# A second MLP run in four segments instead of three, its weight reloads issued by SyncE, and conversion left out of the steps that end block sums

## The chip, the core and the metric

One core of a Trainium2 chip runs the whole program as one launch. The metric is the device time of that launch in microseconds (us). Each kernel was run several times and the median stands for it.

## The reference, cut to what matters

Attention over 4 batches and 8 heads of 576 tokens comes first, then two MLPs over the 2304 tokens with 512 features. The change touches the second MLP (and one detail of the first).

```python
def _moe_ref(x, w_in, w_out):            # first MLP: 512 -> 2048 -> 512
    h = x @ w_in
    g = h - np.tanh(h)
    return (g @ w_out).astype(np.float32)

def _moe2_ref(x, w_gate, w_val, w_out):  # second MLP: 512 -> 1536 -> 512
    gate = 1.0 / (1.0 + np.exp(-(x @ w_gate)))
    val = x @ w_val
    return (gate * val @ w_out).astype(np.float32)
```

## The kernel before, in words

All weights arrive as 64-bit floats and are converted on the chip to a high and a low 32-bit part; every product is then three matmuls (high by high, low by high, high by low).

**First MLP.** 48 steps of two hidden chunks of 128 each, in an order in which each of 6 token blocks of 384 appears once with the first half of the hidden chunks and once with the second half. A step issues `first` (24 matmuls, line 661) and, for an earlier step, `fifth` (24 matmuls into four sums called acc, line 725). When a block's half ends, `sixth` empties the four sums. In the second half it adds the partial result that had been stored: four adds on VectorE (DVE), line 741. The next block's `fifth` needs these four sums free.

**Conversion of the weights.** `Weights.step` takes one item at a time through DVE (four operations, lines 543 to 547), ScalarE (ACT: an absolute value, line 531, and the high part, line 554) and GpSimd (POOL: the low part, line 552, and sums and differences of weights, line 602). Converted weights of the second MLP go through three staging slots to DRAM (`wsc`, stored by SyncE, SP, on line 607). `W.lag` is the number of slots between the operation that frees or fills a buffer and the place in the program where the DMA for it is issued. In the first MLP one item is converted per step. What is left is converted during the second MLP by `convert()`, one piece per slot, four slots per item.

**Second MLP.** Tokens are taken in 3 groups (tau) of 768, hidden features in 6 chunks (fp) of 256. One pair (tau, fp) is here called a unit, so there are 18. A unit has 14 slots: 7 products for each of its two halves m (a scheme with 7 products in place of 8, lines 862 and 895 to 931). A slot's product is 6 matmuls into one of two PSUM banks. ACT or DVE empties the bank; the first product of a half is emptied by ACT (`e<-sum`, line 906), and the next but one product needs that bank. In 12 of the 14 slots a piece of the down projection of the unit before (3 matmuls, line 878) follows the product; slots 12, 13 and 0 come without one, so in the trace the three of them stand as one block of 18 matmuls of line 862, once per unit.

**Reloads.** A unit needs 9 weight tiles of 512 KB from `wsc`, in a ring of 13 buffers. `feed` issues a load as soon as, in program order, the buffer's last user has been issued. In steady state that gives 7 loads in slot 12 and one each in slots 13 and 0. The 7 are called the burst here. They are weights 2 to 8 of the next unit, the first of them wanted in its slot 2. Once the second MLP runs, `feed` issues them from ACT's queue (line 811), between ACT's other instructions. Every DMA also takes one of eight completion semaphores in turn, so it waits until the DMA that stands eight DMAs before it in the program has landed.

**Change of group.** In the last unit of a group the 14 inputs of the next group are made by `x_next` (line 795): two high parts on ACT and two low parts on POOL and DVE in each of 7 slots. In the unit after it the six finished sums leave through `leave` (line 886) and a store to `out`.

Of the kernel before, what the change touches and what calls it, by code (L numbers as in the profile page):

```python
# [7 lines left out]
F32 = mybir.dt.float32  # L8
# [407 lines left out]
TBS = (None, 384, 384)  # L416
# [25 lines left out]
X0_AT = N1 - 4  # L442
X0_STEPS = (X0_AT + 1, X0_AT + 2, X0_AT + 3)

# [188 lines left out]
def mlps(tc, st, xr, x0, W, xs, x2s, out, consts):  # L633
# [158 lines left out]
    def x_make(j, kp, low):  # L792
# [5 lines left out]
          X0_AT + 2: ([(0, 3), (1, 3)], [(6, 0), (6, 1), (7, 0), (7, 1), (5, 0)]),  # L798
          X0_AT + 3: ([], [(5, 1), (4, 0), (4, 1), (3, 0), (3, 1)])}

    loads = [(tau, fp, i) for tau in range(NPAIR) for fp in range(NFP) for i in range(PER_FP)]
    ring, held, issued, spent = [], {}, [0], set()

    def feed():
        while issued[0] < len(loads):
            k = issued[0]
            tau, fp, i = loads[k]
            if (fp, i) not in W.stored or k >= len(ring) and (k < RING_SLOTS or loads[k - RING_SLOTS] not in spent):
                return
            w = W.slot(ring[k % RING_SLOTS])  # L810
            (nc.scalar if s > SLOTS2 // 2 else nc.sync).dma_start(w.bitcast(F32).rearrange("p a c -> p (a c)"), W.wsc[fp][i])  # L811
            held[loads[k]] = w
            issued[0] += 1
# [4 lines left out]
    def convert():  # L818
        while W.made <= W.n:
            highs, lows, mixes, conv = W.step()  # L820
            for f in conv[:2]:
                f()
                yield
            for f in highs + lows:
                f()
            for f in conv[2:]:
                f()
                yield
            for f in mixes:
                f()  # L830
            W.scan()
            if not conv:
                yield
# [13 lines left out]
    def mat(s):  # L847
        g, j = divmod(s, GROUPS2)
        u, m = divmod(g, 2)
        tau, fp = divmod(u, NFP)  # L850
        return tau, fp, m, j

    def product(s):
        tau, fp, m, j = mat(s)
        w = held[tau, fp, j]
        p = banks[s % 2]
        fresh = j in (0, 1, 4)
        for kp in range(2):
            x = xw[PRODUCTS[j], kp]
            for i, (a, c) in enumerate(P3):  # L860
                o = 256 * m + 128 * kp
                T.matmul(p, w[:, a, o:o + 128], x[:, c], start=(fresh and kp == 0 and i == 0),  # L862
                         stop=(kp == 1 and i == 2), skip_group_check=True)
        if m:
            spent.add((tau, fp, j))

    def down():
        if not downs:
            return
        tau, fp, f, key, d, last = downs.pop(0)  # L870
        h, l = res[key]
        w = held[tau, fp, GROUPS2 + f]
        t = key[-1]
        begin = fp == 0 and f == t
        end = fp == NFP - 1 and f != t
        c = slice(128 * d, 128 * d + 128)
        for i, (g, a) in enumerate(((h, 0), (h, 1), (l, 0))):
            T.matmul(sums[3 * t + d], g[:, c], w[:, a], start=(begin and i == 0), stop=(end and i == 2))  # L878
        if last:
            spent.add((tau, fp, GROUPS2 + f))  # L880
        if end:
            return lambda: leave(tau, t, d)

    def leave(tau, t, d):
        o = ob.tile([128, DM], F32, name="o")
        (V.tensor_copy if d % 2 else A.copy)(o, sums[3 * t + d])
        r = TP * tau + TB * t + 128 * d
        nc.sync.dma_start(out[r:r + 128, :], o)
# [10 lines left out]
    def evacuate(s):  # L899
        tau, fp, m, j = mat(s)  # L900
        p = banks[s % 2]
        u = tau, fp
# [27 lines left out]
    def finish(s, u, f, t, q, gate):  # L930
        key = (*u, f, t)
        d = 0 if gate is None else 1
        if d:
            at(s + 1, lambda: G.tensor_mul(q, q, gate))
        c = s + 1 + d
        if f == 0 and t == 1:
            c = max(c, s + 5)
        at(c, lambda: cast(key, q))
        at(c + 1, lambda: lower(key, q))

        def queue():
            for i in range(3):
                downs.append((*u, f, key, i, i == 2 and (f, t) in ((1, 0), (0, 1))))
        order = {(0, 0): 0, (1, 1): 1, (1, 0): 2, (0, 1): 3}[f, t]
        at(SLOTS2 * ((u[0] * NFP) + u[1] + 1) + 3 * order - 1, queue)

    def slot2(s):
        tau, fp, m, j = mat(s)
# [9 lines left out]
        if tau + 1 < NPAIR:  # L958
# [20 lines left out]
    for n in range(N1 + 3):  # L979
# [8 lines left out]
        if 2 <= n < N1 and n not in X0_STEPS:  # L988
# [12 lines left out]
        if n == N1:  # L1001
# [7 lines left out]
            W.lag = 2  # L1009
# [36 lines left out]
    while s < SLOTS2 * NPAIR * NFP:  # L1046
# [19 lines left out]
def tile_attention_then_two_mlps(ctx: ExitStack, tc: tile.TileContext, qT, kT, vP, par, wi, wo, wg, wv, wo2, c_log, ident, out, xs=None):  # L1066
# [5 lines left out]
    x2s = dp.tile([DM, NT], F32, name="x2s")  # L1072
    wsc = [[dp.tile([128, 1024], F32, name=f"wsc{i}_{j}") for j in range(PER_FP)] for i in range(NFP)]
    with tc.manual_schedule():
# [27 lines left out]
        m = mlps(tc, ctx, xr, x0, W, xs, x2s, out, cst)  # L1102
# [75 lines left out]
```

## Time and profile before

| | |
|---|---|
| time, median of 3 runs | 1190.41 us (1187.73 to 1194.6) |
| profiled execution: its own time | 1193.65 us |
| profiled execution: span of the trace | 1191.8 us |
| TensorE matmul busy | 1127.8 us, 95% of the span |
| DVE, ACT, POOL busy | 794.0, 660.6 and 651.7 us |
| mean granted TensorE clock | 0.987 |
| DMA moved | 225.64 MB, mean 189 GB/s |

The span runs from the first to the last instruction. Attention and the biases take about the first 340 us, the first MLP ends near 750 us, and the second MLP fills the rest. A busy share is a mean over all of them, so the stretches have to be read apart.

### The profile page before, as it was taken

The numbers are of one execution on the slowest core, as the hardware profiler recorded it, in microseconds if no ns is written. First come the engines' busy times: TensorE is split into PE (matmuls) and PEld (weight loads), VectorE is DVE, ScalarE is ACT, GpSimd is POOL, SyncE is SP. The second block draws the span as 40 slices with busy tenths as digits, with TensorE's granted clock in tenths as the row PEclk, the third lists the DMA queues.
The fourth block names the chain that finished last, engine by engine and source line by source line (L and its number), as shares of the span: only waits on it lengthen the run. The fifth ranks groups of instructions, "written<-read, shape, count | busy, mean of one in ns | idle before, by whom it ended". The sixth has DMA issues, their size and how long they took to land.

```text
span 1191.8 us, 19819 instructions
## 1 busy us (share of the span) xinstructions
PE 1127.8 (95%) x6968; PEld 980.9 (82%) x6968; DVE 794.0 (67%) x1401; ACT 660.6 (55%) x1313; POOL 651.7 (55%) x588
## 2 busy tenths in 40 slices
PE   5679999999999999999999999988999999999998
PEld 1246676767689999999999999887888998889997
DVE  8979888888579988898899885773242332432222
ACT  7877787778657776677676755433242212421122
POOL 1047777777545655697787954866352223522332
PEclk9889999999999999999999999999999999999999
DMA  6654546363223332367756777976565545664452
GB/s 211 239 185 138 168 141 193 112 200 102 78 72 110 108 107 97 111 230 237 248 190 206 245 249 279 351 292 272 231 241 225 200 159 218 242 228 160 169 232 94
DMA packets 103026, 225.64 MB, mean 189 GB/s; under 512 B 12176, under 2 KB 52368, under 8 KB 102928
## 3 DMA queue, kind: packets, MB, share of 16 engines
q1 hardware_dynamic: 81472, 146.25, 36.8%
q10 hardware_dynamic: 21456, 78.13, 17.1%
q8 instruction: 56, 0.92, 0.3%
q14 instruction: 42, 0.34, 0.1%
HBM read 166.26 MB, written 58.08 MB: 188 GB/s over the span
## 4 chain that ended last, share of the span: by engine, by line
PE 76%; DMA 6%; ACT 5%; DVE 4%; issue 4%; POOL 3%; ACTq 1%; SPq 0%; DVEq 0%; POOLq 0%
PE sum L862 19%; PE acc L725 13%; PE up L661 13%; PE acc L878 8%; PE sc L227 6%; PE pv L319 6%; PE pt L269 6%; PE up L878 3%; DMA w<-wsc 2%; POOL w L552 2%; DMA bsc<-e 1%; ACTq L811 1%; DMA wsc<-w 1%; PE pv L316 1%; PE bt L75 1%
## 5 line engine op out<-in xcount | busy, mean ns | idle before, releaser
L862 PE MATMUL sum<-w,w 128*128 128x384 f32 x1512 | 306.6, 342 | 21.6 <-ACT e L906 12.9
L862 PEld LDWEIGHTS sum<-w,w 128*128 128x128 f32 x1512 | 272.4, 190 | 49.4 <-ACT e L906 19.8
L661 PE MATMUL up<-xt,w 128*128 128x384 f32 x1152 | 208.5, 335 | 0.3 <-DVE t L695 0.3
L661 PEld LDWEIGHTS up<-xt,w 128*128 128x128 f32 x1152 | 200.1, 188 | 2.9 <-issue 2.2
L725 PE MATMUL acc<-gh,w 128*128 128x384 f32 x768 | 195.8, 335 | 4.2 <-DVE o L741 2.5
L259 POOL TENSOR_SCALAR n<-n,rec 128x576 f32<-128x576 f32 x144 | 121.0, 854 | 83.0 <-ACT n L248 41.0
L706 POOL TENSOR_TENSOR gl<-t,gh 128x384 fp32r<-128x384 f32 x96 | 105.3, 1117 | 93.1 <-issue 39.0
L552 POOL TENSOR_TENSOR w<-wu,w 128x512 fp32r<-128x512 f32 x86 | 129.0, 1512 | 29.8 <-ACT w L554 15.0
L725 PEld LDWEIGHTS acc<-gh,w 128*128 128x128 f32 x768 | 138.0, 188 | 6.7 <-ACT xt L651 3.3
L897 POOL TENSOR_TENSOR gl<-e,gh 128x384 fp32r<-128x384 f32 x54 | 57.8, 1074 | 147.0 <-ACT gh L699 146.9
L725 PE MATMUL acc<-gl,w 128*128 128x384 f32 x384 | 128.3, 334 | 0.0
L241 DVE CUSTOM_DVE_ANT_0 n<-sc,bias 128x576 f32<-128x576 f32 x144 | 103.7, 753 | 31.4 <-PE sc L227 26.2
L248 ACT ACTIVATE n<-n,mn 128x576 f32<-128x576 f32 x144 | 111.4, 783 | 8.7 <-DVE mn L241 8.6
L699 ACT CAST gh<-t 128x384 fp32r<-128x384 f32 x114 | 57.7, 515 | 93.3 <-DMA w<-wsc 70.2
L878 PE MATMUL acc<-w,gh 128*128 128x512 f32 x288 | 91.6, 399 | 0.0
L690 ACT ACTIVATE z<-z,c 128x768 f32<-128x768 f32 x48 | 45.2, 941 | 76.3 <-DVE up L689 76.2
L269 PE MATMUL pt<-ident,n 128*128 128x128 f32 x576 | 80.4, 281 | 1.4 <-ACT at L299 1.3
L691 DVE TENSOR_TENSOR t<-up,t 128x768 f32<-128x768 f32 x48 | 45.9, 957 | 53.0 <-ACT t L678 52.4
L319 PE MATMUL pv<-at,vs 128*64 128x320 f32 (+1 forms) x512 | 79.3, 421 | 0.0
L909 DVE TENSOR_TENSOR e<-sum,e 128x384 f32<-128x384 f32 x35 | 19.5, 556 | 89.6 <-ACT e L906 47.2
L923 DVE TENSOR_TENSOR e<-sum,e 128x384 f32<-128x384 f32 x70 | 38.9, 556 | 57.1 <-PE sum L862 57.1
L652 POOL TENSOR_TENSOR xt<-xm,xt 128x384 fp32r<-128x384 f32 x48 | 49.8, 1059 | 44.5 <-ACT xt L651 44.1
(109 smaller groups left out, 2117.2 us busy)
## 6 DMA issues: line engine op xcount, KB each, us to landing
w<-wsc ACTq DMA_DIRECT2D x149, 512.0 KB, 7.8
wsc<-w SPq DMA_DIRECT2D x54, 512.0 KB, 4.9
wraw<-in_wo SPq DMA_DIRECT2D x28, 512.0 KB, 4.3
bsc<-e SPq DMA_DIRECT2D x36, 295.5 KB, 3.1
xm<-xs SPq DMA_DIRECT2D x48, 192.0 KB, 3.3
x2s<-o SPq DMA_DIRECT2D x48, 192.0 KB, 3.7
wraw<-in_wi SPq DMA_DIRECT2D x16, 512.0 KB, 4.2
w<-wsc SPq DMA_DIRECT2D x13, 512.0 KB, 5.6
```

Source lines behind the costliest of these rows:

```text
L227: T.matmul(sc[u, t][:, hf, 0:288], q[r, 128 * s:128 * s + 128], k[r, o:o + 288], start=(i == 0), stop=(i == 2))
L241: V.tensor_tensor_reduce(n.rearrange("p (a b) -> p a b", a=2), s[:, :, 0:288], bias[t].rearrange("p (a b) -> p a b", a=2), -0.125, 3.0e38, ...
L248: A.activation(n, n, AF.Exp, bias=m, scale=-1.0, accum_out=nsum[u, t // 4][:, t % 4:t % 4 + 1])
L259: G.tensor_scalar(n, n, nrec[u, t // 4][:, t % 4:t % 4 + 1], 1.0, ALU.mult, ALU.mult)
L269: T.transpose(pt[:, i], n[:, o:o + 128], ident)
L319: T.matmul(p[0][64 * a:64 * a + 64, 0:N], v[:, c - 1, a], main[:, c - 1, a * N:a * N + N], start=False, stop=(c == 4))
L552: self.nc.gpsimd.tensor_sub(w[:, 1], x, w[:, 0].bitcast(F32))
L661: T.matmul(p[:, 0:TB], w[:, a, 128 * kt:128 * kt + 128], x[:, c], start=(kt == 0 and i == 0), stop=(kt == 3 and i == 2))
L706: G.tensor_sub(l, x[:, j], h.bitcast(F32))
L725: T.matmul(ac[blk][d][:, 0:TB], w[:, a, 128 * d:128 * d + 128], c, start=(begin and j == 0 and i == 0), stop=(end and j == NPR - 1 and i = ...
L862: T.matmul(p, w[:, a, o:o + 128], x[:, c], start=(fresh and kp == 0 and i == 0), stop=(kp == 1 and i == 2), skip_group_check=True)
L878: T.matmul(sums[3 * t + d], g[:, c], w[:, a], start=(begin and i == 0), stop=(end and i == 2))
```

## The change

1. The second MLP runs in four segments (`SEGS`): group 0 with chunks 0 to 2, group 1 with all six chunks, group 2 with all six, group 0 again with chunks 3 to 5. The six sums of the first segment are stored to a DRAM tensor `y2s`; `bring` loads them back in the last unit, and `leave` adds them on DVE. There are still 18 units. The inputs of group 0 are made twice, so there are three changes of group instead of two.
2. All reloads are issued by SP.
3. The steps of the first MLP in which sums of a second half fall due convert nothing (4 steps). So 54 of 68 items, not 58, are made when the second MLP begins, and 14 are left instead of 10.
4. `convert()` yields once more per item: five slots per item in place of four. `W.lag` is 3 slots instead of 2 in the second MLP.
5. Two differences and two input tiles of group 0 are made one step later.

```diff
+SEGS = ((0, 0, 3), (1, 0, NFP), (2, 0, NFP), (0, 3, NFP))
+PAIRS = [(g, tau, fp, fp - lo, hi - lo) for g, (tau, lo, hi) in enumerate(SEGS) for fp in range(lo, hi)]
...
-          X0_AT + 2: ([(0, 3), (1, 3)], [(6, 0), (6, 1), (7, 0), (7, 1), (5, 0)]),
-          X0_AT + 3: ([], [(5, 1), (4, 0), (4, 1), (3, 0), (3, 1)])}
-    loads = [(tau, fp, i) for tau in range(NPAIR) for fp in range(NFP) for i in range(PER_FP)]
+          X0_AT + 2: ([], [(6, 0), (6, 1), (7, 0), (7, 1), (5, 0)]),
+          X0_AT + 3: ([(0, 3), (1, 3)], [(5, 1), (3, 0), (3, 1)]),
+          N1: ([], [(4, 0), (4, 1)])}
+    loads = [(u, i) for u in range(len(PAIRS)) for i in range(PER_FP)]
...
-            (nc.scalar if s > SLOTS2 // 2 else nc.sync).dma_start(w.bitcast(F32).rearrange("p a c -> p (a c)"), W.wsc[fp][i])
+            nc.sync.dma_start(w.bitcast(F32).rearrange("p a c -> p (a c)"), W.wsc[fp][i])
...
             W.scan()
-            if not conv:
-                yield
+            yield
...
+    def leave(g, t, d):
+        tau, lo, hi = SEGS[g]
+        r = TB * t + 128 * d
+        if lo:
+            o = kept.pop((t, d))
+            V.tensor_add(o, sums[3 * t + d], o)
+        else:
+            o = ob.tile([128, DM], F32, name="o")
+            (V.tensor_copy if d % 2 else A.copy)(o, sums[3 * t + d])
+        nc.sync.dma_start(out[TP * tau + r:TP * tau + r + 128, :] if hi == NFP else y2s[r:r + 128, :], o)
+
+    def bring(i):
+        t, d = divmod(i, 3)
+        o = ob.tile([128, DM], F32, name="o") if i < 4 else x0.tile([128, TP], F32, name="xt")[:, 0:DM]
+        nc.sync.dma_start(o, y2s[128 * i:128 * i + 128, :])
+        kept[t, d] = o
...
-            if fp == 1 and m == 0 and j < 4:
-                src_load(tau + 1, j)
-            if fp == 2 and j < 3:
+            if p == n - 3 and m == 1 and j < 4:
+                src_load(SEGS[g + 1][0], j)
+            if p == n - 2 and j < 3:
                 combine(m, j)
-            if fp == NFP - 1 and m == 1:
+            if p == n - 1 and m == 1:
                 x_next(j)
+        elif p == n - 1 and m == 0 and j < 6:
+            bring(j)
...
-        if 2 <= n < N1 and n not in X0_STEPS:
+        if 2 <= n < N1 and n not in X0_STEPS and not any(ends(m) and block(m)[2] for m in due(n - 1, 2)):
             h, low, mixes, conv = W.step()
...
-            W.lag = 2
+            W.lag = 3
```

How instructions move shows at three places. The first is ACT at a unit's end in the steady part, before. Lines 699 and 925 are casts and sigmoids of the hidden features, L811 the weight reloads, L906 the copy that empties a PSUM bank.

```order
L925 ACTIVATE e<-e 128x384
L699 CAST gh<-e 128x384
L811 DMA w_10998<-wsc_2_93 128x1024
L811 DMA w_11000<-wsc_3_94 128x1024
L811 DMA w_11002<-wsc_4_95 128x1024
L811 DMA w_11004<-wsc_5_96 128x1024
L811 DMA w_11006<-wsc_6_97 128x1024
L811 DMA w_11008<-wsc_7_98 128x1024
L811 DMA w_11010<-wsc_8_99 128x1024
L811 DMA w_11020<-wsc_0_100 128x1024
L699 CAST gh<-t 128x384
L811 DMA w_11033<-wsc_1_101 128x1024
```

Now the same place holds no DMA (the same casts and sigmoids, lines 701 and 939, and the copy L920):

```order
L939 ACTIVATE e<-e 128x384
L701 CAST gh<-e 128x384
L701 CAST gh<-t 128x384
L920 COPY e<-sum_9038 128x384
L701 CAST gh<-e 128x384
```

What moved: the nine reloads of a unit have left ACT's program, and the cast of line 701 follows the one before it directly.

The second place is SP in the third unit of the changed kernel, while weights are still being converted: L516 loads raw weights, L609 stores converted ones, L815 reloads.

```order
L609 DMA wsc_5_106<-w_9618 128x1024
L609 DMA wsc_3_104<-w_9619 128x1024
L516 DMA wraw<-in_wg 128x2x256
L516 DMA wraw<-in_wv 128x2x256
L815 DMA w_9745<-wsc_2_67 128x1024
L815 DMA w_9747<-wsc_3_68 128x1024
L815 DMA w_9749<-wsc_4_69 128x1024
L815 DMA w_9751<-wsc_5_70 128x1024
L815 DMA w_9753<-wsc_6_71 128x1024
L815 DMA w_9755<-wsc_7_72 128x1024
L815 DMA w_9757<-wsc_8_73 128x1024
L815 DMA w_9778<-wsc_0_74 128x1024
```

Before, SP's program holds there only raw loads (L514, L518) and stores (L607):

```order
L607 DMA wsc_4_104<-w_9407 128x1024
L607 DMA wsc_2_102<-w_9408 128x1024
L514 DMA wraw<-in_wg 128x2x256
L514 DMA wraw<-in_wv 128x2x256
L607 DMA wsc_1_101<-w_9474 128x1024
L607 DMA wsc_7_107<-w_9475 128x1024
```

What moved: nine reloads per unit now stand in SP's one queue between the stores and raw loads of the conversion, and what comes after them in the program is issued after them.

The third place is DVE in a step of the first MLP that empties four sums of a second half, before. The operations on up and t belong to the activation, those on wu convert weights, and L741 are the four adds.

```order
L689 SCALAR_TENSOR_TENSOR up<-z,up 128x2x384
L547 SCALAR_TENSOR_TENSOR wu<-wraw,wu 128x512
L694 SCALAR_TENSOR_TENSOR up<-q,up 128x2x384
L543 SCALAR_TENSOR_TENSOR wu<-wraw,wu 128x512
L695 COPY_PREDICATED t<-z,up 128x768
L741 TENSOR_TENSOR o<-acc,o 128x384 x4
```

And now:

```order
L693 TENSOR_TENSOR t<-up,t 128x768
L694 SCALAR_TENSOR_TENSOR up<-z,up 128x2x384
L691 SCALAR_TENSOR_TENSOR up<-z,up 128x2x384
L696 SCALAR_TENSOR_TENSOR up<-q,up 128x2x384
L697 COPY_PREDICATED t<-z,up 128x768
L743 TENSOR_TENSOR o<-acc,o 128x384 x4
```

What moved: no operation on wu stands ahead of the four adds in such a step.

## Rows read from the trace of the kernel before

**Rows 1.** The page, part 1: busy time, share of the span, instructions.
```profile
PE 1127.8 (95%) x6968; PEld 980.9 (82%) x6968; DVE 794.0 (67%) x1401; ACT 660.6 (55%) x1313; POOL 651.7 (55%) x588
```

**Rows 2.** Waits of TensorE from 500 us on: total, times, longest.
```profile
PE sum L862 <- ACT e L906: 12.9, 13, 2.8
PE sum L862 <- DVE e L923: 6.6, 4, 2.2
PE acc L725 <- DVE o L741: 2.5, 3, 1.2
```

**Rows 3.** Timeline of TensorE, line 862: start, length, count of matmuls.
```profile
743.54 7.49 PE L862 MATMUL sum<-w,w 128*128 128x384 f32 x42
...
774.82 3.30 PE L862 MATMUL sum<-w,w 128*128 128x384 f32 x18
...
801.67 3.30 PE L862 MATMUL sum<-w,w 128*128 128x384 f32 x18
...
832.76 3.30 PE L862 MATMUL sum<-w,w 128*128 128x384 f32 x18
...
880.57 3.69 PE L862 MATMUL sum<-w,w 128*128 128x384 f32 x18
...
935.11 3.30 PE L862 MATMUL sum<-w,w 128*128 128x384 f32 x18
...
1030.51 3.69 PE L862 MATMUL sum<-w,w 128*128 128x384 f32 x18
...
1082.55 3.30 PE L862 MATMUL sum<-w,w 128*128 128x384 f32 x18
...
1153.69 3.30 PE L862 MATMUL sum<-w,w 128*128 128x384 f32 x18
...
1176.89 2.26 PE L862 MATMUL sum<-w,w 128*128 128x384 f32 x12
```

**Rows 4.** Timeline, 1020 to 1062 us, ACT's DMA queue and TensorE (idle before, releaser).
```profile
1030.70 3.58 ACTq L811 DMA_DIRECT2D w<-wsc  x7
1034.38 0.51 ACT L795 CAST w<-xt 128x384 fp32r<-128x384 f32 x1 [3.86 <-DMA w<-wsc]
...
1036.90 1.33 PE L862 MATMUL sum<-w,w 128*128 128x384 f32 x6 [2.01 <-DVE e L923]
```

**Rows 5.** Windows: length, busy of each engine, granted clock, DMA share, GB/s.
```profile
1036.00:1064.00 28.00, 26.74 (x129) 24.44 (x129) 8.94 (x16) 7.98 (x17) 10.46 (x10) 0.94 0.57 213
```

**Rows 6.** Timeline of ACT, 770 to 830 us.
```profile
775.02 3.73 ACTq L811 DMA_DIRECT2D w<-wsc  x7
...
782.87 0.48 ACT L906 COPY e<-sum 128x384 f32<-128x384 f32 x1 [2.48 <-DMA w<-wsc]
...
801.87 4.08 ACTq L811 DMA_DIRECT2D w<-wsc  x7
...
818.79 1.20 ACT L554 CAST w<-wu 128x512 fp32r<-128x512 f32 x2 [4.50 <-POOL wu L602]
```

**Rows 7.** The chain that ended last, 797 to 810 us: start, length, what.
```profile
802.51 7.23 DMA wsc<-w
```

**Rows 8.** Timelines of the first MLP, 606 to 617 us, TensorE then DVE.
```profile
606.83 4.32 PE L661 MATMUL up<-xt,w 128*128 128x384 f32 x24
612.36 0.59 PE L725 MATMUL acc<-gh,w 128*128 128x384 f32 x2 [1.21 <-DVE o L741]
616.63 4.32 PE L661 MATMUL up<-xt,w 128*128 128x384 f32 x24
...
609.90 0.92 DVE L543 SCALAR_TENSOR_TENSOR wu<-wraw,wu 128x512 int32<-128x512 int32 x1
...
611.67 1.94 DVE L741 TENSOR_TENSOR o<-acc,o 128x384 f32<-128x384 f32 x4
```

**Rows 9.** DMA issues: of 1100 to 1115 us, then of the whole span.
```profile
w<-wsc ACTq DMA_DIRECT2D x9, 512.0 KB, 8.2
...
wsc<-w SPq DMA_DIRECT2D x54, 512.0 KB, 4.9
```

More of the change, by code (lines that the diff above doesn't have):

```diff
@@ L630, in zip_run, with mlps @@
                 x[i]()
-def mlps(tc, st, xr, x0, W, xs, x2s, out, consts):
+def mlps(tc, st, xr, x0, W, xs, x2s, y2s, out, consts):
     nc = tc.nc
@@ L806, in feed @@
             k = issued[0]
-            tau, fp, i = loads[k]
+            u, i = loads[k]
+            fp = PAIRS[u][2]
             if (fp, i) not in W.stored or k >= len(ring) and (k < RING_SLOTS or loads[k - RING_SLOTS] not in spent):
@@ L849, in mat @@
         u, m = divmod(g, 2)
-        tau, fp = divmod(u, NFP)
-        return tau, fp, m, j
+        return u, m, j
     def product(s):
-        tau, fp, m, j = mat(s)
-        w = held[tau, fp, j]
+        u, m, j = mat(s)
+        w = held[u, j]
         p = banks[s % 2]
@@ L864, in product @@
         if m:
-            spent.add((tau, fp, j))
+            spent.add((u, j))
     def down():
@@ L869, in down @@
             return
[L870 to L875, printed above, removed]
+        u, f, t, d, last = downs.pop(0)
+        g, tau, fp, at_, n = PAIRS[u]
+        h, l = res[u, f, t]
+        w = held[u, GROUPS2 + f]
+        begin = at_ == 0 and f == t
+        end = at_ == n - 1 and f != t
         c = slice(128 * d, 128 * d + 128)
-        for i, (g, a) in enumerate(((h, 0), (h, 1), (l, 0))):
-            T.matmul(sums[3 * t + d], g[:, c], w[:, a], start=(begin and i == 0), stop=(end and i == 2))
+        for i, (x, a) in enumerate(((h, 0), (h, 1), (l, 0))):
+            T.matmul(sums[3 * t + d], x[:, c], w[:, a], start=(begin and i == 0), stop=(end and i == 2))
         if last:
-            spent.add((tau, fp, GROUPS2 + f))
+            spent.add((u, GROUPS2 + f))
         if end:
[L882 to L888, printed above, removed]
+            return lambda: leave(g, t, d)
+    def leave(g, t, d):
[8 more added lines that the diff above has]
+        nc.sync.dma_start(out[TP * tau + r:TP * tau + r + 128, :] if hi == NFP else y2s[r:r + 128, :], o)
+    kept = {}
+    def bring(i):
[3 more added lines that the diff above has]
+        kept[t, d] = o
     grp = {}
@@ L899, in evacuate @@
     def evacuate(s):
-        tau, fp, m, j = mat(s)
+        u, m, j = mat(s)
         p = banks[s % 2]
-        u = tau, fp
         if j == 0:
@@ L930, in finish @@
     def finish(s, u, f, t, q, gate):
-        key = (*u, f, t)
+        key = u, f, t
         d = 0 if gate is None else 1
@@ L942, in queue @@
             for i in range(3):
-                downs.append((*u, f, key, i, i == 2 and (f, t) in ((1, 0), (0, 1))))
+                downs.append((u, f, t, i, i == 2 and (f, t) in ((1, 0), (0, 1))))
         order = {(0, 0): 0, (1, 1): 1, (1, 0): 2, (0, 1): 3}[f, t]
-        at(SLOTS2 * ((u[0] * NFP) + u[1] + 1) + 3 * order - 1, queue)
+        at(SLOTS2 * (u + 1) + 3 * order - 1, queue)
     def slot2(s):
-        tau, fp, m, j = mat(s)
+        u, m, j = mat(s)
+        g, tau, fp, p, n = PAIRS[u]
         W.tick()
@@ L957, in slot2 @@
             f()
-        if tau + 1 < NPAIR:
-            if fp == 1 and m == 0 and j < 4:
-                src_load(tau + 1, j)
-            if fp == 2 and j < 3:
+        if g + 1 < len(SEGS):
+            if p == n - 3 and m == 1 and j < 4:
+                src_load(SEGS[g + 1][0], j)
+            if p == n - 2 and j < 3:
                 combine(m, j)
-            if fp == NFP - 1 and m == 1:
+            if p == n - 1 and m == 1:
                 x_next(j)
+        elif p == n - 1 and m == 0 and j < 6:
+            bring(j)
     def x_next(j):
@@ L1045, in mlps @@
     conv = convert()
-    while s < SLOTS2 * NPAIR * NFP:
+    while s < SLOTS2 * len(PAIRS):
         slot2(s)
@@ L1072, in tile_attention_then_two_mlps @@
     x2s = dp.tile([DM, NT], F32, name="x2s")
+    y2s = dp.tile([2 * TBS[2], DM], F32, name="y2s")
     wsc = [[dp.tile([128, 1024], F32, name=f"wsc{i}_{j}") for j in range(PER_FP)] for i in range(NFP)]
@@ L1101, in tile_attention_then_two_mlps @@
         xr, x0 = (ctx.enter_context(tc.tile_pool(name=n, bufs=k)) for n, k in (("p2r", 2), ("p2x0", 4)))
-        m = mlps(tc, ctx, xr, x0, W, xs, x2s, out, cst)
+        m = mlps(tc, ctx, xr, x0, W, xs, x2s, y2s, out, cst)
         def tail(h):
```

## The prediction

> **What bounds the kernel now.** I began with the busy shares [rows 1]: TensorE is at 95%, no other engine above 67%. So other engines matter only where they make TensorE wait, and what can be won at all is TensorE's idle time and the time it runs at a lower granted clock. The table of TensorE's waits says where it idles in the second half [rows 2]: it waits for the copy on ACT that empties a PSUM bank (12.9 us in 13 waits), for DVE's adds that do the same (6.6 us) and, in the first MLP, for the four adds that empty the block sums (2.5 us in 3 waits). No row of that table names a DMA: a reload is never what TensorE itself waits for.
>
> The idle time alone is too small, since after an idle stretch the clock is lower. So I measured whole units: each unit has one block of 18 matmuls, and the distance from block to block is the unit's length [rows 3]. The last two blocks stand 1176.89 - 1153.69 = 23.2 us apart. That is the floor: 14 products of 1.05 us and 12 down pieces of 0.70 us make 23.1. The first block of interest starts at about 743.54 + 5 x 1.05 = 748.8. Over 17 units the second MLP then loses, against 23.2 a unit:
>
> - 748.8 to 832.76, 3 units, weights still being converted: 84.0 - 69.6 = 14.4
> - 832.76 to 880.57, 2 units: 1.4
> - 880.57 to 935.11, 2 units, change of group and the sums' leaving: 8.1
> - 935.11 to 1030.51, 4 units: 2.6
> - 1030.51 to 1082.55, 2 units, the other change of group: 5.6
> - 1082.55 to 1153.69, 3 units: 1.5
>
> Together 33.6 us. What causes it is seen in a change of group [rows 4]. ACT's queue issues the burst of seven loads in 3.58 us; the eighth has to wait for the completion of an earlier load, and the next cast on ACT starts only when that DMA has landed, after 3.86 us idle. ACT works in order, so the inputs of the next group come late, DVE behind them comes late, and TensorE stands for 2.01 us. In the 28 us that follow the mean granted clock is 0.94 [rows 5], so about an eighth of them, some 3 us, passed at the lower level, 1.2 instead of 2.4 GHz, and cost about 1.7 us more. In the conversion the same thing happens [rows 6]: seven issues at 775.02, then ACT's copy of a bank at 782.87, released by a DMA; again at 801.87. At 818.79 the cause is another: ACT waits 4.50 us for POOL's arithmetic on weights.
>
> **The change, part by part.**
>
> *Reloads off ACT.* The nine issues per unit, and the waits between them, go to SP, which computes nothing. The nine steady units (1.4 + 2.6 + 1.5 = 5.5 us) should fall nearly to the floor; I leave 0.5. The two changes of group (13.7 us) keep their work: 14 casts of 0.51 us [rows 4] on ACT, and as many subtractions shared by POOL and DVE, in the seven slots of half a unit, some 12 us. I leave 1 us each, 2 in all. In the conversion I count the loss of 774.82 to 801.67 (26.85 - 23.2 = 3.65) and half of that of 801.67 to 832.76 (31.09 - 23.2 = 7.9, half is 3.8, for the burst at 801.87) to this cause; 7 of the 14.4 stay. What hides the loads afterwards: the first weight of a burst is wanted after the three products of the block (3.2 us), two down pieces and one product, 5.6 us after the issue, and it lands 3.7 us after (1030.70 to 1034.38) [rows 4]. So there is a margin of 1.9 us. Without it, each microsecond of lateness is one of TensorE.
>
> *What SP's one queue now carries.* During the conversion, raw loads and converted stores stand among the reloads, in two ways. A store issued behind a burst lands late: nine loads have a median of 8.2 us to landing [rows 9], the first lands after 3.7, so the last at about 12.7. A store that lands in 4.9 alone [rows 9], and took 7.23 beside a burst in the other queue [rows 7], may take 10 to 15. The staging slot stays taken and ACT's high part waits. By the order of the changed kernel that happens to two of the stores, each with two slots of normal slack. Conversely two bursts stand directly behind two stores and a raw load, some 3 x 1.1 us of transfer (from 8.2 - 3.7 over four loads) against the margin of 1.9. I put 1 us on each of the four, 4 in all; bounds 0 (the slack takes it) and 12 (3 each).
>
> The Trainium skill, "DMA: Bandwidth & Descriptors", "Issuing engines are not separate DMA queues", says that issuing DMAs on several engines only saves the sequencer's issue time, usually small beside the DMA. Read so, taking the loads off ACT would return little; here the trace differs, because 3.58 us of issues and 3.86 us of waiting stand in ACT's program [rows 4]. By the rule alone the steady and group terms would stay as they are.
>
> *Slower conversion, spread wider.* Group 0 stops after chunk 2, so chunks 3 to 5 are wanted at unit 6 instead of unit 3, and an item may take five slots (8.8 us) instead of four (7.0). POOL gets a quarter more time for each, which should ease waits like that of 818.79; but 14 items are left instead of 10. Of the 7 us I keep 5 (bounds 2, if the pace cures it, and 10, if each item costs as before: 7 x 14/10). The store's lag grows from two slots to three, which takes back most of the added room for a staging slot's round trip.
>
> *A third change of group.* The first one now falls into the conversion, where POOL has both the subtractions and the weights. It has no ACT issues, so it need not cost what the two old ones cost; it cannot be free either. I take 3 (bounds 0 and 6.9, half of 13.7).
>
> *First MLP.* In the four steps of line 741 that are changed, DVE loses its four conversion operations, of which one alone takes 0.92 us just ahead of the adds [rows 8]. The stalls are 1.21 us and less, so they should vanish: -2.5 [rows 2]. The four items come back as part of the 14.
>
> *The rest.* TensorE has the same count of products. Six stores and six loads of 256 KB and four of 384 KB are 4.6 MB beside 225 and lie under the products. The last six sums now all leave through DVE, by an add where a copy stood; the chain at the end grows by about 0.3. The two moved differences and input tiles cost nothing as long as POOL is idle where they go; bound 1.
>
> **Sum.** Losses after: 0.5 + 2 + 5 + 3 + 4 + 0.3 = 14.8 instead of 33.6, so -18.8; with the first MLP -21.3. The profiled execution took 1193.65 us, so 1172.3; it lies 3.2 above the median of the runs, 1190.41, which gives 1169.
>
> **The rivals.**
>
> *The conversion eats it.* Two-part items follow each other through three staging slots exactly where the first change of group lies. With all three uncertain terms at their upper bounds (10, 6.9, 12 instead of 5, 3, 4) the sum is 16.9 us worse: -4.4, and 1186. Halfway is 1178. For it: POOL's 4.50 us wait [rows 6]; against: five slots per item. Chance of 1176 to 1184: 0.20.
>
> *ACT's issues only hid the transfers.* The stall of a change of group [rows 4] ends when a DMA lands. If TensorE would then wait for the same load, the 19.2 us of steady units and group changes stay, and what is left is the first MLP (-2.5) and the 2 us that the slower pace takes off the conversion: -4.5, so 1186. Against it: steady units lose no more than half a microsecond each while the same bursts run [rows 3], and no wait of TensorE is on a DMA [rows 2]. The skill's rule above would give this time. Chance 0.09, together with other ways of ending within 0.5%, which is about what a measurement of this kernel can tell from no change.
>
> *Slower: one queue, in order.* SP waits for a low part from POOL before it issues a store, and the burst behind it waits too. This can happen in five units of conversion and three in which sums leave. Without the 4 us for the queue, the change gives 25.3; so it turns into a loss when each of these 8 units waits longer than 3.2 us, idle and slow clock together. At 4 us each, 32 us, the time is 1197. The Trainium skill, same page, "Queues, rings and completion order", supports the shape of it: SP and ACT own one row of rings each, and descriptors of one ring are taken in order. No run here shows yet how far that delays a burst. For it: the store of 7.23 us [rows 7]; against: the loads are in the queue 5.6 us ahead. Chance 0.06.
>
> *Better.* Slack takes up all new terms: conversion 2, group change 0, queue 0 give -31, and 1159. Chance of below 1162: 0.03.
>
> **How the numbers follow.** My forecast, 1169, stands for the case 1162 to 1176 with chance 0.62. Faster by over 0.5% (below 1184.5): 0.62 + 0.20 + 0.03 = 0.85; within 0.5%: 0.09; slower: 0.06. The range 1158 to 1183 takes in the likeliest case and the second and leaves out the two that end near or above the old time.
>
> **What would show it.** In the profile after: no DMA issue on ACT in the second MLP; steady blocks of 18 matmuls 23.2 to 23.4 us apart; the two later changes of group within 2 us of the floor; adds of the block sums in the first MLP without a wait before them in the four steps; a total loss in the first five units below 15 us. Wrong would be: waits of TensorE on a reload, ACT's line for the high parts waiting on a store (the queue), POOL's row full in the third and fourth unit (the conversion), or group changes that still cost 4 us a unit without ACT's issues (then ACT's queue was not the cause).

## The result and the profile after

The changed kernel takes 1173.66 us (median of 4 runs, 1170.99 to 1175.9) against 1191.24 us for the kernel before in the same runs: the ratio is 0.9852, with a 95% interval of 0.9816 to 0.9888. It is faster by 1.5%. The profiled execution took 1173.8 us, its span is 1172.0 us.

The busy shares on the page have hardly moved (compare [rows 1]):

```profile
PE 1123.8 (96%) x6968; PEld 983.2 (84%) x6968; DVE 816.5 (70%) x1422; ACT 666.6 (57%) x1327; POOL 661.2 (56%) x595
```

TensorE's table of waits from 500 us on has (compare [rows 2]; the operations are the same, only the line numbers have moved: L927 is the sigmoid on ACT that empties a bank, L933 and L937 are adds on DVE that do):

```profile
PE sum L864 <- ACT e L927: 4.4, 1, 4.4
PE sum L864 <- DVE t L933: 2.1, 1, 2.1
PE sum L864 <- DMA w<-wsc: 1.8, 1, 1.8
PE sum L864 <- DVE t L937: 1.1, 1, 1.1
PE sum L864 <- DVE e L929: 1.0, 1, 1.0
```

The 12.9 us of waits on ACT's bank copy are gone, and one wait of 4.4 us on ACT's other bank-emptying operation, the sigmoid, has come; the waits in the first MLP are gone; a wait on a reload is new. The timeline of the unit blocks shows where the time is lost now (compare [rows 3]):

```profile
736.72 7.47 PE L864 MATMUL sum<-w,w 128*128 128x384 f32 x42
...
773.03 3.30 PE L864 MATMUL sum<-w,w 128*128 128x384 f32 x18
...
828.02 3.33 PE L864 MATMUL sum<-w,w 128*128 128x384 f32 x18
...
878.04 3.30 PE L864 MATMUL sum<-w,w 128*128 128x384 f32 x18
...
901.24 3.30 PE L864 MATMUL sum<-w,w 128*128 128x384 f32 x18
...
947.64 3.67 PE L864 MATMUL sum<-w,w 128*128 128x384 f32 x18
...
971.21 3.30 PE L864 MATMUL sum<-w,w 128*128 128x384 f32 x18
...
1157.16 2.26 PE L864 MATMUL sum<-w,w 128*128 128x384 f32 x12
```

The unit's length is the distance from block to block, and 23.2 us is the floor that the prediction found. From 878.04 on, 12 units take 279.1 us, 0.7 more than 12 times 23.2. The two changes of group there cost 0.37 us each (947.64 to 971.21 is 23.57). Before, the same kinds of units lost 5.5 and 13.7 us. All the rest is lost earlier. The first block begins at 736.72 + 5.25 = 742.0; the unit to 773.03 loses 7.9 us, the two to 828.02 lose 8.6, the two to 878.04 lose 3.6. That is 20.1 us in these first five units (called the conversion stretch here), where the kernel before lost 14.4 + 1.4 = 15.8.

The whole balance between the two profiled executions: 1.4 us are scatter of the unchanged part (the first of the paired steps of the first MLP starts at 345.60 instead of 347.03); the first MLP from there to the first block is 5.4 us shorter (396.4 instead of 401.8); the second MLP loses 20.8 instead of 33.6, which is 12.8; the end after the last block is the same (14.8 and 14.9 us). Together 19.7, and the executions differ by 19.85.

The chain that ended last shows the first of the three losses, the one of 4.43 us idle (start, length, what):

```profile
745.33 10.32 DMA wsc<-w
755.65 0.02 issue
755.67 0.04 ACTq L556
...
755.75 0.07 ACT w L556
...
756.27 0.49 ACT e L927
...
756.81 2.29 PE sum L864 x6
```

A store of converted weights needs 10.32 us. The high part of the next item (L556) waits on ACT for its staging slot, and the sigmoid that empties a bank (L927) stands behind it in ACT's order. After the idle time six matmuls take 2.29 us, and the windows show the granted clock for the three stretches:

```profile
742.00:773.00 31.00, 26.19 (x121) 23.12 (x120) 21.90 (x30) 8.73 (x18) 21.19 (x16) 0.89 0.82 308
773.00:828.00 55.00, 50.40 (x241) 45.29 (x240) 42.62 (x56) 25.49 (x52) 45.38 (x34) 0.94 0.84 309
828.00:878.00 50.00, 48.20 (x241) 44.35 (x240) 27.69 (x44) 17.04 (x34) 33.20 (x27) 0.97 0.81 308
878.00:948.00 70.00, 70.00 (x364) 65.09 (x363) 25.98 (x45) 19.32 (x40) 26.51 (x27) 1.00 0.61 236
```

A mean of 0.89 means that about a fifth of that window passed at 1.2 GHz; the idle time that TensorE's table names for it is 4.4 of the 7.9 us. In the second stretch, the first change of group, the chain runs through DVE:

```profile
791.02 1.78 DVE wu L549
...
793.19 1.16 DVE w L797
794.35 1.43 DVE wu L545
...
797.05 2.84 DVE xt L792 x2
...
801.08 1.23 DVE wu L547
```

The conversion (wu) and the subtractions of the change (w, xt) alternate on DVE without a gap, and the banks' adds stand between them. POOL has no gap there either, from 789.66 to 802.02 us. In the third stretch TensorE waits 1.80 us for a reload that took 5.63 us (829.84 to 835.47). It is the first of a burst, and SP had issued two stores, a partial sum and a raw load in the 3.3 us ahead of it.

### The profile page after: what moved, and what is told of

Its sections match the earlier page's. It is cut to its first block, busy times and chain, and to the rows that moved or that the text cites. A ratio compares the mean times of both kernels' runs of the same rounds, so it can differ in the third digit from the quotient of the medians.

```text
span 1172.0 us, 19922 instructions
## 1 busy us (share of the span) xinstructions
PE 1123.8 (96%) x6968; PEld 983.2 (84%) x6968; DVE 816.5 (70%) x1422; ACT 666.6 (57%) x1327; POOL 661.2 (56%) x595
## 4 chain that ended last, share of the span: by engine, by line
PE 86%; DMA 4%; DVE 3%; ACT 3%; issue 2%; POOL 1%; SPq 0%; DVEq 0%; ACTq 0%; POOLq 0%
PE sum L864 22%; PE acc L727 16%; PE up L663 16%; PE acc L880 8%; PE sc L227 6%; PE pv L319 6%; PE pt L269 5%; PE up L880 4%; DMA bsc<-e 1%; ACT y L62 1%; PE pv L316 1%; ACT e L86 1%; DMA wsc<-w 1%; PE bt L75 1%; PE pf L273 1%
## 5 line engine op out<-in xcount | busy, mean ns | idle before, releaser
L937 DVE TENSOR_TENSOR e<-sum,e 128x384 f32<-128x384 f32 x70 | 38.8, 556 | 56.1 <-PE sum L864 55.9
L269 PEld LDWEIGHTS pt<-ident,n 128*128 128x128 f32 x576 | 63.8, 142 | 12.6 <-issue 11.4
```

The source lines that it names most:

```text
L269: T.transpose(pt[:, i], n[:, o:o + 128], ident)
```

## The experiments

Each kernel was timed in turn with the kernel before. "Loss" is that of the second MLP in the profiled execution, worked out as above: from the first block to the last, less 17 times 23.2 us. "ACT on store" is ACT's waiting for a staging slot, the row `ACT w <- DMA wsc<-w` of its waits from 716 to 940 us. Both are read from one execution each, while the executions of one kernel lie up to 8 us apart (e7: 1175.54 to 1183.59), so a difference of a few us between two losses is not resolved by itself. The kernel before differs by up to 3 us between the rows as well, so times are compared by their ratios.

| kernel | median us | ratio to before (95%) | loss | ACT on store |
|---|---|---|---|---|
| changed kernel | 1173.66 | 0.9852 (0.9816 to 0.9888) | 20.8 | 9.1 |
| e1, reloads on ACT | 1208.05 | 1.0152 (1.0125 to 1.0178) | 55.4 | 4.6 |
| e2, before with reloads on SP | 1174.24 | 0.9865 (0.9840 to 0.9891) | 15.4 | 3.6 |
| e3, pause at the change | 1183.49 | 0.9956 (0.9936 to 0.9976) | 28.6 | 25.9 |
| e4, conversion in the sum steps | 1173.09 | 0.9856 (0.9826 to 0.9886) | 15.5 | 18.6 |
| e5, two rings | 1169.99 | 0.9854 (0.9836 to 0.9872) | 17.9 | 7.8 |
| e6, stores on POOL | 1179.34 | 0.9930 (0.9913 to 0.9946) | 25.0 | 17.8 |
| e7, three segments | 1177.43 | 0.9922 (0.9892 to 0.9952) | 22.0 | 18.4 |
| e8, inputs as before | 1175.74 | 0.9899 (0.9878 to 0.9920) | 20.1 | 8.8 |
| r9, six slots | 1167.06 | 0.9812 (0.9769 to 0.9854) | 13.4 | 21.3 |
| r10, e3 + e5 + later input loads | 1177.70 | 0.9892 (0.9860 to 0.9924) | 24.9 | 22.8 |
| r11, r10 with six slots | 1163.10 | 0.9774 (0.9751 to 0.9798) | 9.9 | 21.1 |
| r12, r11 with four staging slots | 1161.05 | 0.9753 (0.9739 to 0.9767) | 7.4 | none |

**e1: everything but the queue.**
```diff
-            nc.sync.dma_start(w.bitcast(F32)...
+            (nc.scalar if s > SLOTS2 // 2 else nc.sync).dma_start(w.bitcast(F32)...
```


> The changed kernel with the reloads of the second MLP issued from ACT's queue again; segments, pace, lag and the steps without conversion stay. Theory (ACT's issues and waits cost the time): the steady units and the two late changes of group lose again what they lost before, about 18.5 us (1.4 + 8.1 + 2.6 + 5.6 + 1.5 less the 0.7 that is left), so about 1192 us if the conversion stretch stays as it is, a little less if the stores in a queue of their own land earlier. Rival (the new order of units and the slower pace did it, the queue is indifferent): 1174 us, within 4.

It is slower than the kernel before by 1.5%, and by 34 us than the changed kernel; the last twelve units lose 28.6 us (885.65 to 1192.65) where the changed kernel loses 0.7. The direction is the theory's and the rival is out. The size is larger than either number. ACT's own timeline and the chain show why at the place of the largest loss: eight issues are spread over 10 us and the ninth follows at 897.40, because four of the nine each wait until an input load on SP's queue has landed, the last of which takes 10.06 us. In the trace each of the four has the same completion semaphore as the load that it waits for.

```profile
885.84 10.05 ACTq L815 DMA_DIRECT2D w<-wsc  x8
895.94 0.51 ACT L701 CAST gh<-t 128x384 fp32r<-128x384 f32 x1 [12.64 <-DMA w<-wsc]
...
887.26 10.06 DMA xt<-x2s
...
897.37 0.04 issue
897.40 0.33 ACTq L815
...
897.77 0.49 ACT e L920
...
898.30 1.97 PE sum L864 x5
```

By the times in the two traces, ACT's issues in the second MLP were held until an earlier DMA had landed 13 times here, 26.8 us together, and 6 times, 9.6 us together, in the kernel before.

So the other parts of the change, without the queue's move, cost 19 us (1208.05 against 1188.74 for the kernel before in the same runs).

**e2: the queue alone.**
```diff
-            (nc.scalar if s > SLOTS2 // 2 else nc.sync).dma_start(w.bitcast(F32)...
+            nc.sync.dma_start(w.bitcast(F32)...
```


> The kernel before with one line changed: reloads from SP's queue. Three segments, four slots per item, lag 2, conversion in every step. Theory: the stretch behind the conversion falls to the floor, 15 to 18 us less than before; the conversion stretch loses its ACT issues but gets stores behind bursts, so its 14.4 us become anything from 10 to 20: 1171 to 1181 us. Rival (only the four segments leave room for the conversion): the conversion stretch gets worse by more than 10 us and the whole gain is under 8, above 1183 us.

One changed line gives the same time as the whole change (the intervals of the ratios overlap nearly fully), inside the theory's band. Its waits in the first MLP are about those of before ([rows 2] has the first of them), and its second MLP loses 15.4 us, 14.7 of them in the first five units, less than the changed kernel:

```profile
PE sum L862 <- ACT e L906: 5.9, 1, 5.9
PE acc L725 <- DVE o L741: 2.5, 3, 1.2
...
PE acc L725 <- ACT w L795: 1.8, 1, 1.8
```

**e4: the four items converted in the first MLP after all.** The condition that skips `W.step` is taken out.
```diff
-        if 2 <= n < N1 and n not in X0_STEPS and not any(ends(m) and block(m)[2] for m in due(n - 1, 2)):
+        if 2 <= n < N1 and n not in X0_STEPS:
```


> The changed kernel, converting in the four steps of the first MLP in which the block sums fall due, as before the change; 10 items are then left for the second MLP instead of 14. Theory: TensorE waits for the four adds again, 3 to 4 us in the first MLP; but the conversion in the second MLP has four items less and ends 20 slots earlier, which takes 0 to 6 us off its 20. So 1170 to 1177 us. Rival (the skipped steps are worth what the first MLP gained, and the items cost nothing later): 1177 us.

The ratio is that of the changed kernel. The first MLP's waits of 2.5 us on the adds are back and the first block starts 5.2 us later (747.1), while the loss after it is 5.3 us smaller (15.5). What the first MLP gains by leaving four items out, the second pays for them, as far as one execution can tell. The theory is borne out, the rival (1177) is not.

**e8: the moved differences and inputs.** The table `X0` as before the change.

> The changed kernel with the two differences and two input tiles of group 0 made where they were made before the change. Theory (the moved work freed the wait of 1.0 us before the last block sums of the first MLP): that wait comes back, TensorE's waits in the first MLP sum to about 1 us instead of 0, and the time grows by 1 us, 1173 to 1176 us. Rival (this move cost and saved nothing, as I had predicted): 1173.7 us and no wait in the first MLP.

TensorE's wait on ACT's input tile is back with 1.0 us, as the theory had it. In the time, the intervals overlap; this size is not resolved.

**e7: group 0 in one piece.**
```diff
-SEGS = ((0, 0, 3), (1, 0, NFP), (2, 0, NFP), (0, 3, NFP))
+SEGS = ((0, 0, NFP), (1, 0, NFP), (2, 0, NFP))
...
-            yield
+            if not conv:
+                yield
```
(with the input loads and differences at chunks 1 and 2, and no `bring`)

> The changed kernel with group 0 in one piece again: three segments and four slots per item; reloads on SP, no conversion in the sum steps and lag 3 stay. Theory (the segments only make room, and the room is not what was short): the conversion stretch loses between 14 and 24 us, 1169 to 1179 us, so within 5 us of the changed kernel. Rival (the room counts): with 14 items at four slots each the weights come too late for their unit and TensorE waits for reloads, above 1182 us.

The loss is 22.0 us, 1.2 more than with four segments and five slots, and the two profiled executions lie 2.75 us apart; no wait of TensorE is on a reload, so the rival is out. How little the segments and the fifth slot are worth is less sure: the ratios lie 0.7% apart, some 8 us, and their intervals just miss each other. Against e2, too, e7 is slower (0.9922 and 0.9865, intervals that just miss each other): with three segments, the skipped steps, the lag and the moved inputs together gain nothing.

**e3: no conversion during the first change of group.**
```diff
-        if s > SLOTS2 // 2:
+        if s > SLOTS2 // 2 and not 2 * SLOTS2 + GROUPS2 <= s < 3 * SLOTS2:
             next(conv, None)
```


> The changed kernel, with no piece of conversion in the seven slots of the first change of group; it ends seven slots later, still ahead of where the weights are wanted. Theory (DVE has the group's subtractions and the conversion at once in those slots): the 8.6 us lost between 773 and 828 us fall to 2 to 4, so 1167 to 1170 us. Rival (the change of group costs this by itself, as before the change): 1173 us, the loss stays within 2 us of 8.6.

Both theories missed: 1183.5 us. The change itself is cured, as this theory said: the two units from 770.04 to 817.27 lose 0.8 us, where the changed kernel lost 8.6. But the timeline of TensorE shows two new stalls:

```profile
770.04 3.30 PE L864 MATMUL sum<-w,w 128*128 128x384 f32 x18
...
793.25 3.67 PE L864 MATMUL sum<-w,w 128*128 128x384 f32 x18
...
817.27 3.71 PE L864 MATMUL sum<-w,w 128*128 128x384 f32 x18
...
836.14 2.29 PE L864 MATMUL sum<-w,w 128*128 128x384 f32 x6 [7.39 <-ACT e L927]
...
893.60 2.29 PE L864 MATMUL sum<-w,w 128*128 128x384 f32 x6 [9.32 <-ACT e L927]
```

The chain ahead of the second has the same members as the one of the changed kernel at 745 us:

```profile
880.50 11.93 DMA wsc<-w
...
892.53 0.62 ACT w L556
893.15 0.40 ACT e L927
893.55 0.04 issue
893.60 2.29 PE sum L864 x6
```

The conversion now stands seven slots later against the reloads. ACT's waits on stores are 25.9 us instead of 9.1. I formed a second theory: the staging slots are the trouble, and the burst ahead of a store is what makes it late.

**e5: the burst taken apart** (nine buffers for the products' weights, four for the down weights, each filled in its own order).
```diff
-    loads = [(u, i) for u in range(len(PAIRS)) for i in range(PER_FP)]
+    loads = [[(u, i) for u in range(len(PAIRS)) for i in part] for part in (range(GROUPS2), range(GROUPS2, PER_FP))]
...
+        for q, (lo, n) in enumerate(((0, 9), (9, 4))):
```


> The changed kernel with the 13 reload buffers split into nine for the products' weights and four for the down weights, so that the loads of a unit go out one per slot from slot 8 on instead of seven in slot 12. Theory (a store of converted weights behind a burst lands after 10 to 12 us and holds ACT's next high part, and so a bank): the waits of ACT's high parts on a store shrink below 3 us in all and the stretch of 20 us loss falls to 8 to 14, 1162 to 1168 us. Rival (the conversion is limited by DVE and POOL work, the queue's order is not what counts): the loss stays within 3 us of 20, 1171 to 1177 us.

The ratio is that of the changed kernel, and the stretch loses 17.2 us of the whole 17.9: at the edge of the rival's band. (The median, 1169.99, lies between the two bands, but the kernel before, timed beside it, was 3 us faster too: 1188.23.) One half of the burst's part is borne out: the wait on a reload is gone, and the third stretch, now 830.71 to 877.14, is at the floor, where the changed kernel lost 3.6. With it, the three runs with two rings of nine and four buffers (e5, r10, r11) have no wait of TensorE on a reload. The other half is not: the wait in the second unit, 5.1 us on the same sigmoid, stays, behind a store of 11.07 us. There no burst stands ahead of the store: between 738 and 758 us the changed kernel moves raw loads, seven single reloads, block sums, inputs and stores, 6.97 MB with the DMA engines 96% busy.

**e6: the stores in a queue of their own.**
```diff
-        self.nc.sync.dma_start(self.wsc[at[0]][at[1]], ...
+        (self.nc.gpsimd if self.lag == 3 else self.nc.sync).dma_start(self.wsc[at[0]][at[1]], ...
```


> The changed kernel with the stores of converted weights issued from POOL's queue in the second MLP; the bursts stay. Theory (the store's place behind the burst in SP's queue is what makes it late): waits of ACT's high parts on a store shrink, the stall of 4.4 us at the second unit goes, 1164 to 1170 us, if POOL does not lose more than some 0.5 us per issue. Rival (stores and loads share the same transfer capacity, the queue makes no difference to the landing): landing stays at 10 us beside a burst, 1172 to 1178 us.

Both bands missed: 1179.34 us. ACT waits on the stores for 17.8 us, and the whole is slower. In the median the stores take 5.4 us to landing from POOL's queue and 4.3 from SP's in the changed kernel (740 to 880 us). But the run does not settle whether the place in SP's queue makes a store late, because POOL's program takes its place. The store behind the first stall lands in 6.68 us instead of 10.32, and is issued 4.2 us later, behind POOL's own arithmetic:

```profile
744.01 1.73 POOL w L554
745.74 1.16 POOL gl L912
746.89 1.28 POOL t L948
748.17 0.61 POOL wu L604
...
749.55 6.68 DMA wsc<-w
```

So the stall stays, 4.0 us.

**r9: six slots per item.** One more `yield` in `convert()`.

> The changed kernel with six slots per item of conversion in place of five; the weights are still made before their unit. Theory (in the conversion stretch the transfers, 308 GB/s with the DMA engines over 80% busy, pile up in bursts, and the staging slots wait): fewer stores and raw loads per unit, but the two large stalls stand at fixed places (the reload of the next group's inputs in the first unit, the first change of group), so the 20 us fall only to 14 to 19: 1167 to 1173 us. Rival (the mean load of transfers is what counts): below 10 us lost, under 1164 us.

1167.06 us, at the theory's lower end; the loss is 13.4. The interval of the ratio overlaps that of the changed kernel, so the gain of the sixth slot alone is not resolved. TensorE now waits 1.3 us on ACT's bank copies in all, although ACT waits 21.3 us on stores: most of that waiting lies where no bank is due. Its longest wait is now on a reload, 2.7 us.

**r10 and r11: three edits, then with six slots.** r10 is e3, e5, and the next group's input loads moved out of the first unit:
```diff
-            if p == n - 3 and m == 1 and j < 4:
+            if g and p == n - 3 and m == 1 and j < 4 or not g and p == n - 2 and m == 0 and j < 4:
                 src_load(SEGS[g + 1][0], j)
```
(the differences then follow in that unit's second half)

> The changed kernel with three edits: two rings of reload buffers, no conversion in the seven slots of the first change of group, and the four input loads of the next group taken out of the first unit, where raw loads, reloads and stores already fill the DMA engines, into the second. Theory: the stall in the first units is caused by those transfers (7.9 us lost), the one at the change by DVE's doubled work (8.6 us), and the spread reloads keep the stores of the later units from landing late as they did when the pause stood alone; so 20 falls to 4 to 10 us and the time to 1158 to 1165 us. Rival (the loss moves on to where the conversion then stands, as with the pause alone): 1169 us or more.

> The three edits together and six slots per item. Theory: as the kernel with the three edits, with 0 to 3 us less, since stores and raw loads get thinner: 1156 to 1163 us. Rival (a longer conversion meets more bursts): slower than the three edits alone by 2 us or more.

r10 refuted its theory: 24.9 us lost, the rival's case. r11, the same with six slots, loses 9.9 and ends at the upper edge of its band, but not as its theory said: the sixth slot takes off 14.6 us, not 0 to 3. ACT waits on stores equally long in both (22.8 and 21.1 us), but TensorE waits for ACT to empty a bank for 16.3 us in r10 and for 5.0 in r11.

**r12: a fourth staging slot**, taken from the products' reload buffers.
```diff
-X_SLOTS, T_SLOTS, RING_SLOTS = tuple(range(14)), (14, 15), 13
+X_SLOTS, T_SLOTS, RING_SLOTS = tuple(range(14)), (14, 15), 12
...
-        for q, (lo, n) in enumerate(((0, 9), (9, 4))):
+        for q, (lo, n) in enumerate(((0, 8), (8, 4))):
```


> The three edits and six slots per item, and one of the reload buffers of the products given to the staging of converted weights: four staging slots instead of three, eight product buffers instead of nine. Theory (a high part waits on ACT for the store of the item before it, because three slots make two-part items overlap): ACT's 21 us of waits on stores fall below 6, the two stalls that are left in the conversion stretch (28.7 and 25.0 us units) go, and with them 5 to 7 us: 1156 to 1160 us. Rival (the stores are only pushed along, or eight product buffers bring the reloads too late): 1161 us or more, with waits of TensorE on reloads.

ACT's waits on stores are gone, and with them every wait of TensorE on ACT; this was the theory. The stores did not land sooner: 7.6 us in the median (740 to 880 us), 7.3 in r11 and 4.3 in the changed kernel. The gain is smaller than the theory said, 2.5 us of loss, since a reload is now late once, in a unit of 27.8 us. With 1161.05 us and a wait on a reload, this half of the rival is met to the letter. TensorE's whole table of waits from 480 us on:

```profile
PE sum L866 <- DMA w<-wsc: 2.5, 1, 2.5
PE sum L866 <- DVE e L939: 0.3, 1, 0.3
```

r12 is the fastest of all, 0.9753 of before; its interval overlaps that of r11.

## Why the prediction was right, and which terms were not

*The direction and the cause.* The forecast of 1169 was 5 us low and the range held. That the reloads in ACT's program were what mattered is shown by e2 (the move alone gives as much as the whole change) and e1 (without it the rest is a loss). The rival that the issues only hid the transfers is out: TensorE waits once, 1.8 us, on a reload, and in e2 not at all. That the time came so near is in part luck. For the profiled execution the sum said 1172.3 and 1173.8 was measured, but the conversion stretch lost 8.1 us more than allowed, and most of this was made up elsewhere: 1.8 us less in the steady units and late changes, 2.9 us more from the first MLP, 0.3 at the end and 1.4 of scatter. The 3.2 us that the forecast took off to get from the profiled execution to the median were not there after the change, where the two agree (1173.8 and 1173.66).

*What in ACT's program cost the time.* Here the prediction misread [rows 4]. It counted 3.58 us of issues and 3.86 us of waiting for a DMA. But the 3.86 us are ACT's idle time, and the seven issues lie inside them (1030.70 to 1034.28). The cast at 1034.38 follows the last of them directly, and the eighth issue comes after it:

```profile
1034.49 0.94 ACTq L811 DMA_DIRECT2D w<-wsc  x1
...
L811 ACTq DMA_DIRECT2D w<-wsc x149: 326/445/1226, 744.8 to 1157.0; - x149
```

The second line has the shortest, median and longest issue in ns; the 149 add up to 74.0 us, 7.4 of them beside other work of ACT. Waits of an issue for an earlier landing are real, as at 782.87 and behind the store of 802.51 ([rows 6], [rows 7]), but there were six, 9.6 us in all, and only two of them, 2.9 us, behind the conversion stretch. By the same count, 18 issues stood 42.3 us until TensorE had used their buffer for the last time, with all that follows in ACT's program behind them. So in the steady units and the late changes of group the issues and these waits for a buffer held ACT, and landings hardly did. How TensorE's loss divides between the two was not tested.

*Steady units and late changes of group.* Foreseen 0.5 + 2 of 19.2 us left; measured 0.7. The Trainium skill ("DMA: Bandwidth & Descriptors", "Issuing engines are not separate DMA queues") says that issuing DMAs from several engines saves only the issuing sequencer's time, which is usually small beside the DMA. If that time is taken as small, all 19.2 would have stayed. The traces differ in two ways: issuing was not small for ACT, about 0.5 us an issue and nine of them in each unit of 23.2 us, and what an issue waits for, a buffer or a landing, held ACT's program too. TensorE waited on that engine. In e1, waits for landings came on top.

*First MLP.* Foreseen -2.5, measured -5.4 by distance. The table of waits that the term was taken from counts 2.5 us for the adds alone; two waits on ACT, 0.6 and 1.0 us, vanished as well, and the prediction had put the moved inputs, which e8 connects with the second of them, at no cost and no gain. The rest of the 5.4 is not told apart. The price of the four items was inside the conversion term, not beside it; in e4's one execution they take back all of it.

*The conversion stretch is the step that failed.* The prediction allowed 5 + 4 + 3 = 12 us for pace, queue and the third change of group, where before it was 15.8; measured are 20.1, against its own sign of less than 15. The change of group took 8.6, above its upper bound of 6.9. The prediction had POOL as the engine that would be short; the chain runs through DVE, though POOL had no gap there either. That the conversion beside the change is the cause is shown by e3: without it the two units lose 0.8 us. Late stores and reloads took 7.9 + 3.6 = 11.5 instead of 4. The late reload is the one the prediction described, a burst behind stores and a raw load, and with the burst taken apart it goes (e5). For the stores, the mechanism, a store that holds a staging slot and so ACT, is the one it named (r12 removes it). What makes them late is not the burst in SP's order alone: the first stall has no burst ahead of it, and e5 keeps it. The likeliest cause is that the transfers together leave the DMA engines hardly idle, 96% busy there, but no run shows it, and the load does not set the loss: r11 has them 98% busy from 738 to 758 us and loses 0.9 us in that unit instead of 7.9. What the runs do show is that with a fourth slot stores of 7.6 us hold nothing. The order within one row of rings, for which the prediction named the Trainium skill ("DMA: Bandwidth & Descriptors", "Queues, rings and completion order"), is neither contradicted nor tested by itself. What the slower pace should have saved on POOL's waits does not show as a term of its own.

*Where the expected gain went.* In the changed kernel, segments, pace and skipped steps are worth nothing that the intervals resolve beside the queue's move (e2 against the changed kernel). The profiled executions show how they cancel: the changed kernel's first block starts 5.6 us earlier than e2's, and its conversion stretch loses 5.4 us more. With the three other edits, a sixth slot per item is worth 14.6 us (r11 against r10). Only four segments leave the time for it by count: 14 items at six slots are 84 slots, and with three segments the last chunk is wanted in slots 70 to 83. No run tried six slots with three segments.

What stays open: what makes the stores late, and why five slots with the three edits (r10) lose 15 us more than six. ACT waits as long on stores in both; the profile says that in r10 the waits fall ahead of the emptying of a bank, and no run moved the phase alone.

## What to carry to other kernels

Look not at how busy an engine is that issues DMAs, but at who stands behind the issue in its program: the issue itself, and whatever it has to wait for (a free buffer, an earlier landing), are paid by every instruction after it. When a profile gives an engine's idle time and names a DMA as its end, look whether the engine was issuing in that time. Before several parts of a change are credited, run the largest alone; here one line gained as much as all of them. And where buffers are few, measure the round trip of a buffer under load, up to 11 us here where the median was 4.3, before setting a pace by it.

## What the runs showed of the hardware that was not expected

The two differences of a change of group on DVE (line 792, 128x384, both operands in SBUF) took 2.91 us together at 796.97 us, while POOL worked without a break, and 1.84 us at 1084.62 us, where POOL had a gap of 0.74 us; that POOL is the cause was not tested, and the DMA engines were busier there too (57% from 796 to 800 us, 1% from 1084 to 1087). The stores of 512 KB landed no earlier in the median from POOL's queue (5.4 us, in e6) than from SP's (4.3 us, in the changed kernel) in the same stretch, though the slowest took 8.6 us against 11.1.
